# A branch is moved behind the row numbers and the first gather of a routed expert layer, which are then done on a guess

## The chip, the cores and the metric

One Trainium2 chip, one of its cores. The metric is the time of the whole kernel on the device in microseconds (us), the median of several runs.

The core has five engines that work side by side, each in the order of its own instructions: PE (matrix multiplications), DVE (vector operations), ACT (activations and scaled copies), POOL (general vector work, and here the indirect DMAs that gather and scatter rows) and SP (which here issues most of the other DMAs). They wait for one another through semaphores.

## The reference

Attention in blocks, then a layer of eight experts that each take exactly 576 of the 4608 rows.

```python
# q, k, v: 8 x 8 heads x 576 x 64;  block-causal mask of 64
attn = softmax(where(mask, q @ k.T / 8, -1e9)) @ v
x = attn.transpose(0, 2, 1, 3).reshape(4608, 512)

logits = x @ w_gate                     # 4608 x 8
order = argsort(-logits.flatten())      # best pairs of row and expert first
for idx in order:                       # greedy, an expert is full at 576 rows
    tok, e = idx // 8, idx % 8
    if assigned[tok] >= 0 or counts[e] >= 576: continue
    assigned[tok] = e; counts[e] += 1
for e in range(8):
    rows = x[assigned == e]
    out[assigned == e] = relu(rows @ w1[e]) @ w2[e]   # 512 -> 1024 -> 512
```

## The kernel before

The first 330 us or so are attention, which writes x to DRAM as two halves of 16 bits (a high and a low part, 1024 numbers a row). Then come the experts in the order in which they fill up, not in the order of their numbers. For the k-th of them (k from 0 to 7) the class `Moe` does these steps, and those of k+1 lie beside the matrix work of k:

- `route`: a search for the threshold above which exactly 576 pairs lie. A round (`rounds`) counts the pairs above three candidates with DVE and ACT (tiles `jk`, `ja`), sums the counts over the partitions on PE (`tot`) and narrows the interval. For k = 0 it makes 6 rounds, then assumes that the interval is already narrow enough; `bi` says whether that guess is wrong, and a region under `If` does eight more rounds in that case. For k > 0 it makes 14 rounds. `choose` then gives the expert's number (`ei`, as an integer `eidx`) and the mask of its rows (`MM`).
- The end of `route` and `invert`: two scans over the mask, sums on PE, and a row number for every place (`ix`).
- `weights`: SP reads `eidx` into a register and loads this expert's w1 and w2 in eight pieces into six buffers `raw`. ACT makes the high half of each piece, and DVE (k < 2, first four pieces) or POOL (the rest, L991) the low half. A piece may be loaded when the low half of the piece six before it is done.
- `gather`: five indirect DMAs on POOL, m = 0 to 4, fetch 128 rows each (64 for m = 4) into tiles `xg`. `flip` transposes them into X: for k < 2 on PE (`xt`), from k = 2 on by a DMA that SP issues (L1058).
- `ffn`: h = W1 X (L1083), in two halves of the rows, 256 and 320; HH and HL are the high and low half of relu(h); y = HH, HL times W2 (L1109, L1113). POOL scatters the result to its rows (`out_dram`).

A class `Sched` decides the order of the instructions ahead of time. Each step is a generator that yields the engine it needs, an estimated duration in ns, and the events it has to follow; the planner keeps a clock for each engine and takes the step that can start first. It knows only costs and events that are written out; what a tile of a pool waits for is added afterwards as semaphores when a buffer is taken again. `gather` takes `xg` from a pool of five buffers.

The branch for k = 0 is written out by hand: a register load on DVE, PE and ACT, a comparison, and the region (L863, L864). Behind it come the scans (L874), the row numbers, the load of `eidx` on SP (L969) with the first weights, and the first gather. `m_gt` is a small tile that POOL clears behind the first gather (L1032) and DVE writes before its first low half (L979). `m_dg` (L780) is a gather into a tile that nobody reads.

Of the kernel before, what the change touches and what calls it, by code (L numbers as in the profile page):

```python
# [596 lines left out]
class Moe:  # L597
    def __init__(s,tc,nc,ctx,sc,L,xd,w1,w2,out):
        s.tc,s.nc,s.sc,s.L,s.xd,s.w1,s.w2,s.out=tc,nc,sc,L,xd,w1,w2,out
        s.NT=xd.shape[0]; s.D=w1.shape[1]; s.E=w1.shape[0]; s.F=w1.shape[2]; s.CAP=s.NT//s.E; s.C=s.NT//P  # L600
# [4 lines left out]
        s.ab=s.cp.tile([P,1],F32,name="m_ab")
        s.vm=s.cp.tile([P,s.C],F32,name="m_vm"); s.nP=s.cp.tile([P,s.C,s.E],F32,name="m_nP"); s.Lr=s.cp.tile([P,s.C,s.E],F32,name="m_Lr")
        N=s.C*s.E; s.PAD=s.CAP*s.E//P
        s.PB,s.P2=[s.cp.tile([P,N+s.PAD],F32,name=n) for n in ("m_PB","m_P2")]
# [86 lines left out]
    def route(s,k):  # L695
# [10 lines left out]
        SC=rp.tile([P,2,C+1],F16,tag="SC",name=f"SC{k}")  # L706
        eidx=rp.tile([P,1],I32,tag="eidx",name=f"eidx{k}")
        (V if k else nc.gpsimd).memset(SC[:,:,0:1],0.0)
        if last:

# [4 lines left out]
        else:  # L715
# [38 lines left out]
            def rounds(t0,t1):  # L754
                nonlocal lo,nw,PBx,base
                for t in range(t0,t1):
# [91 lines left out]
            else:  # L848

                cg=rp.tile([P,1],F16,name="m_cg",bufs=1); bad=rp.tile([P,2],F32,name="m_bad",bufs=1); bi=rp.tile([P,1],I32,name="m_bi",bufs=1)  # L850
                yield from rounds(0,s.TB)
# [9 lines left out]
                V.scalar_tensor_tensor(bi,tot[:,0:1],float(s.CAP),bad[:,0:1],op0=OP.not_equal,op1=OP.max)  # L861
                ET=mybir.EngineType
                rv=nc.values_load(bi[0:1,0:1],engines=(ET.DVE,ET.PE,ET.Activation),min_val=0,max_val=1)  # L863
                with s.tc.If(rv>0):  # L864
# [6 lines left out]
        nm=1 if last else 2  # L871
        yield D,106*nm
        for i in range(nm):
            V.tensor_tensor_scan(SC[:,i,1:],s.ones[:,:C],MM[:,i],0.0,op0=OP.mult,op1=OP.add)  # L874
        def full():
# [47 lines left out]
    def invert(s,k,L16,h2):  # L923
# [32 lines left out]
        V.tensor_copy(ix,ps[:,:5])  # L956
        sc.set(tk)
        sc.add(s.gather(k,ix),s.PR['gather'],sc.now); sc.set(('ix',k))
        if k==0: sc.add(s.late(),0,sc.now)
        if k==0:  # L960
# [3 lines left out]
            sc.free[T]=max(sc.free[T],sc.now)+213*s.NWU+1500  # L964
        s.ix[k]=ix
    def weights(s,k,eidx):

        nc=s.nc; wp=s.wp; sc=s.sc
        e=nc.sync.value_load(eidx[0:1,0:1],min_val=0,max_val=s.E-1)  # L969
        yield S,1000,('ffn',k-2)  # L970
# [22 lines left out]
        for dst,src,nd,wd in ((W,s.w1,4,1024),(Y,s.w2,8,512)):  # L993
            g=1024//wd
            for d in range(0,nd,g):
# [8 lines left out]
                else: yield S,25,'hw'  # L1004
                if k>1 or n!=4: raw=wp.tile([P,1024],F32,tag="raw",name=f"raw{k}_{wd}_{d}",bufs=6)
                nc.sync.dma_start(out=raw.rearrange("p (g f) -> p g f",g=g),in_=src[bass.ds(e,1),d*P:(d+g)*P,:].rearrange("o (g p) f -> p (o g) f",p=P))  # L1006
                hi=dst[:,0,d:d+g].rearrange("p g f -> p (g f)"); lw=dst[:,1,d:d+g].rearrange("p g f -> p (g f)")
# [12 lines left out]
    def gather(s,k,ix):  # L1020
        nc=s.nc; fp=s.fp; sc=s.sc
        tl=[]
        for m in range(5):
# [4 lines left out]
            nc.gpsimd.indirect_dma_start(out=xg[:n],out_offset=None,in_=s.xd,in_offset=bass.IndirectOffsetOnAxis(ap=ix[:n,m:m+1],axis=0))  # L1028
            sc.soft(728,('xg',k,m))
            sc.nolat()  # L1030
            if k==m==0:
                s.gt=s.rp.tile([P,1],F32,name="m_gt",bufs=1); nc.gpsimd.memset(s.gt,0.0); sc.set(('gt',0))  # L1032
            if m==4: sc.set(('gi',k))
# [144 lines left out]
```

## Time and profile before

| what | value |
|---|---|
| median of 3 runs | 759.99 us (757.54 to 761.68) |
| the profiled execution | 753.41 us, of it 751.6 us the span that the profile shows |
| mean granted clock of PE | 0.982 |
| busy share of the span | PE 94%, DVE 73%, ACT 68%, POOL 51% |

The span is the stretch from the first to the last instruction of the core. The page divides it into 40 slices of 18.8 us; the hand-over from attention to the experts lies in the slices from 325 us on, where PE falls to 6 and 3 tenths. Rows of a timeline give start, duration, engine, line, operation, the tile written and the tiles read, the count of instructions drawn together, and in brackets the idle time of the engine before it and what ended it. SPq, DVEq and so on are the sequencers of the engines. "DMA to landing" is the time from the issue of a transfer until its data have arrived.

### The profile page before, as it was taken

What the parts mean: (1) busy time and instruction counts of PE and PEld (TensorE: products, weight loads), DVE (VectorE), ACT (ScalarE), POOL (GpSimd) and SP (SyncE); (2) the same over time, 40 slices, a digit from 0 to 9 for tenths busy, and PEclk for the clock granted to TensorE, in tenths of its full rate; (3) what the DMA queues carried; (4) which work ended last, traced back from release to release, by engine and by line L of the source; (5) the groups of instructions that cost most, each with busy time, mean ns of one, the idle gap of its engine ahead of it and who ended that gap; (6) DMA issues with size and microseconds to landing.
All of it is one profiled execution on the core that took longest, in us unless ns stands there. A gap on an engine that the chain in (4) does not pass through costs nothing.

```text
span 751.6 us, 18263 instructions
## 1 busy us (share of the span) xinstructions
PE 705.6 (94%) x6314; PEld 455.0 (61%) x6314; DVE 550.6 (73%) x2224; ACT 508.7 (68%) x1378; POOL 380.3 (51%) x455
## 2 busy tenths in 40 slices
PE   5999999999899999637999999999999999999997
PEld 3666776667576766416446647557476475574753
DVE  6999989798887979868989969779587595120210
ACT  5887889888696877427648497694965947474211
POOL 6876564645655562213334276391761834796002
PEclk9999999999999999858999999999999999999999
DMA  9999999999999999745045095673935917993001
GB/s 192 173 200 188 205 214 179 237 179 238 181 238 173 228 202 181 179 141 188 2 169 182 24 305 88 227 167 100 256 80 176 203 38 238 221 260 88 22 15 49
DMA packets 273517, 124.48 MB, mean 166 GB/s; under 512 B 247296, under 2 KB 256512, under 8 KB 273424
## 3 DMA queue, kind: packets, MB, share of 16 engines
q1 hardware_dynamic: 267504, 104.37, 64.9%
q0 software_dynamic: 5920, 18.95, 8.3%
q8 instruction: 49, 0.80, 0.5%
q14 instruction: 44, 0.36, 0.2%
HBM read 71.39 MB, written 18.87 MB: 120 GB/s over the span
## 4 chain that ended last, share of the span: by engine, by line
PE 47%; DMA 3%; issue 3%; ACT 2%; POOL 1%; DVE 1%; SPq 0%; POOLq 0%; ACTq 0%
PE h L1083 24%; PE y L1109 18%; PE y L1113 3%; DMA raw<-in_moe_w_dram 2%; DMA xg<-x,ix 1%; PE pe L944 1%; POOL xg L1028 1%; ACT ja L735 0%; DMA out_dram<-yo,ix 0%; PE xt L1049 0%; PE tot L797 0%; SPq L1006 0%; ACT raw L985 0%; POOL W L991 0%; POOL out_dram L1099 0%
## 5 line engine op out<-in xcount | busy, mean ns | idle before, releaser
L1083 PE MATMUL h<-X,W 128*128 128x320 f16 (+3 forms) x1536 | 194.6, 287 | 0.0
L393 ACT ACTIVATE P<-psb,m 128x576 f32<-128x576 f32 (+8 forms) x288 | 149.5, 546 | 36.9 <-DVE m L389 35.1
L1083 PEld LDWEIGHTS <-W 128*128 128x128 f16 x1536 | 142.6, 98 | 41.9 <-issue 2.6
L991 POOL TENSOR_TENSOR W<-raw,W 128x1024 f16<-128x1024 f32 x56 | 118.4, 2138 | 80.9 <-ACT W L989 61.5
L1109 PE MATMUL y<-W,HH 128*128 128x512 f16 x512 | 152.4, 379 | 0.0
L385 DVE TENSOR_REDUCE m<-psb 128x1 f32<-128x576 f32 (+8 forms) x288 | 124.5, 479 | 10.5 <-PE psb L367 9.8
L437 PE MATMUL psb<-mident,P 128*128 128x128 f32 x800 | 105.5, 279 | 5.3 <-DVE Xf L454 1.9
L437 PEld LDWEIGHTS psb<-mident,P 128*128 128x128 f32 x800 | 85.8, 141 | 24.1 <-ACT P L393 6.8
L1109 PE MATMUL y<-W,HL 128*128 128x512 f16 x256 | 97.0, 379 | 0.0
L1069 ACT ACTIVATE HH<-h 128x320 f16<-128x320 f32 (+3 forms) x128 | 51.7, 411 | 66.9 <-PE h L1083 65.4
L487 PE MATMUL psb<-PT,V 128*64 128x448 f32 (+5 forms) x776 | 96.7, 389 | 0.0
L1099 POOL DMA_INDIRECT out_dram<-yo,ix x40 | 39.1, 978 | 113.3 <-ACT yo L1091 73.9
L367 PE MATMUL psb<-kT,qT 128*64 128x512 f16 (+7 forms) x640 | 85.5, 292 | 3.4 <-DMA qT<-q 1.6
L1071 DVE SCALAR_TENSOR_TENSOR HL<-h,HH 128x320 f16<-128x320 f32 (+3 forms) x128 | 57.2, 453 | 39.1 <-ACT HH L1069 38.6
L418 ACT ACTIVATE PT<-psb 128x512 f32<-128x512 f32 (+1 forms) x157 | 79.4, 580 | 7.3 <-PE psb L437 5.5
L367 PEld LDWEIGHTS <-qT 128*64 128x64 f16 x1280 | 60.8, 110 | 38.5 <-issue 16.6
L1109 PEld LDWEIGHTS <-HH 128*128 128x128 f16 x512 | 46.6, 97 | 52.6 <-issue 1.5
L367 PE MATMUL psb<-kS,qT 128*64 128x512 f16 (+7 forms) x640 | 77.9, 287 | 0.0
L985 ACT ACTIVATE raw<-raw 128x512 f32<-128x512 f32 x112 | 67.8, 627 | 10.6 <-DMA raw<-in_moe_w_dram 10.4
L487 PEld LDWEIGHTS psb<-PT,V 128*64 128x64 f32 x776 | 48.5, 137 | 34.6 <-issue 24.5
L989 ACT ACTIVATE W<-raw 128x512 f16<-128x512 f32 x112 | 68.1, 626 | 0.0
L393 ACT ACTIVATION_READ_ACCUMULATOR P<-psb,m 128x1 f32 x288 | 64.7, 225 | 0.0
(232 smaller groups left out, 1009.7 us busy)
## 6 DMA issues: line engine op xcount, KB each, us to landing
raw<-in_moe_w_dram SPq DMA_DIRECT2D x64, 512.0 KB, 5.0
x<-XR SPq DMA_DIRECT2D x8, 1152.0 KB, 6.7
kn<-in_k_dram SPq DMA_DIRECT2D x15, 576.0 KB, 7.5
qn<-in_q_dram SPq DMA_DIRECT2D x15, 576.0 KB, 7.7
V<-in_v_dram SPq DMA_DIRECT2D x64, 128.0 KB, 2.8
V<-in_v_dram SPq DMA_DIRECT2D x16, 64.0 KB, 2.9
xg<-x,ix POOLq DMA_INDIRECT x40, 4.7
out_dram<-yo,ix POOLq DMA_INDIRECT x40, 3.5
```

Source lines behind the costliest of these rows:

```text
L367: nc.tensor.matmul(ps[64 * h:64 * h + 64, o + a:o + e], lhsT=A[:, h, 64 * i:64 * i + 64], rhs=K[:, h, a:e], start=st, stop=not st)
L385: nc.vector.tensor_reduce(m[:, 0, c:c + 1], ps[:, o:o + 64 * (i + 1)], axis=AX.X, op=OP.max)
L393: nc.scalar.activation(Pt[:, s.OFF[i]:s.OFF[i] + 64 * (i + 1)], ps[:, o:o + 64 * (i + 1)], AF.Exp, bias=m[:, 1, c:c + 1], scale=s.ESC, acc ...
L418: s.nc.scalar.activation(out, in_, AF.Copy)
L437: nc.tensor.transpose(ps[:, a], s.Pb[n % s.NP][:, s.OFF[i] + 128 * j:s.OFF[i] + 128 * j + P], s.ident)
L487: nc.tensor.matmul(ps[64 * h:64 * h + 64, 64 * (i0 - b0):64 * (b1 - b0)], lhsT=vn[:, j, 2 * (n % 2) + h, :], rhs=pt[:, s.PTI[(j, i0)]:s.PT ...
L985: nc.scalar.activation(raw[:,x],raw[:,x],AF.Copy,scale=s.WS)
L989: nc.scalar.activation(hi[:,x],raw[:,x],AF.Copy)
L991: nc.gpsimd.tensor_tensor(lw,raw,hi,op=OP.subtract)
L1071: nc.vector.scalar_tensor_tensor(HL[:,f,ts],ps,0.0,HH[:,f,ts],op0=OP.max,op1=OP.subtract)
L1083: nc.tensor.matmul(ps,lhsT=W[:,a,d,f*P:f*P+P],rhs=X[:,4*(d//2)+d%2+l,ts],start=(d==0 and n==0),stop=(d==3 and n==2))
L1109: if m<4: nc.tensor.matmul(ps,lhsT=Z[:,f,m*P:m*P+P],rhs=Y[:,a,f],start=(f==n==0),stop=(f==7 and n==2))
```

## The change

- For k = 0 the scans, the sums on PE, the row numbers and the first gather no longer stand behind the branch. `eidx` is copied ahead of it, and SP issues the first four weight loads with it.
- The branch (register load and `If`) stands behind `ix`, and now also runs on POOL and SP. POOL's first gather and the clearing of `m_gt` stand ahead of its `If`. The region, for a wrong guess, makes the eight rounds, and then all of this once more: `eidx`, the loads, scans, row numbers and first gather.
- The first gather of k = 0 has a tile of its own (`m_xg0`); the pool `xg` has four buffers in place of five.
- Three small DVE operations (`full`, `used`, `eight`) stand behind the branch; the gather into `m_dg` is gone; the register loads of `eidx` leave out a range check.

```diff
@@ Moe.__init__
+        s.xg0=s.cp.tile([P,1024],F16,name="m_xg0"); s.bi=s.cp.tile([P,1],I32,name="m_bi"); s.e0=s.cp.tile([P,1],I32,name="m_e0")
@@ route, rounds
-                    if k==0 and t==3:
-                        dg=rp.tile([32,1024],F16,name="m_dg",bufs=1)
-                        nc.gpsimd.indirect_dma_start(out=dg,out_offset=None,in_=s.xd,in_offset=bass.IndirectOffsetOnAxis(ap=s.it[:32,P-1:P],axis=0))
@@ route, k == 0
-                yield D,150
+                V.tensor_copy(eidx,ei)
                 V.tensor_tensor(bad[:,0:1],m1[:,6:7],m1[:,1:2],op=OP.not_equal)
+                sc.busy(D,150)
+                yield D,212
+                scans()
+                yield D,100
                 V.scalar_tensor_tensor(bi,tot[:,0:1],float(s.CAP),bad[:,0:1],op0=OP.not_equal,op1=OP.max)
-                ET=mybir.EngineType
-                rv=nc.values_load(bi[0:1,0:1],engines=(ET.DVE,ET.PE,ET.Activation),min_val=0,max_val=1)
-                with s.tc.If(rv>0):
+                yield T,80,'rt'
+                tk=sc.take(); ps=s.ps.tile([P,512],F32,tag="rt",name=f"po{k}")
+                ranks(ps)
+                wg=s.weights(k,eidx)
+                sc.add(wg,s.PR['weights'],sc.now)
+                s.wgo()
+                def redo(e,L16,h2,q):
                     for x in rounds(s.TB,s.NS): pass
                     end()
                     for x in choose(s.NS,0,False): pass
-                for x in (D,T,A): sc.busy(x,1500)
-                yield D,150
-                load()
+                    V.tensor_copy(eidx,ei)
+                    s.fetch(eidx)
+                    scans()
...
@@ invert
+        if k==0:
+            ET=mybir.EngineType
+            rv=nc.values_load(s.bi[0:1,0:1],engines=(ET.DVE,ET.PE,ET.Activation,ET.Pool,ET.SP),min_val=0,max_val=1,skip_runtime_bounds_check_because="a comparison wrote it, so it is 0 or 1")
+            rows=lambda: nc.gpsimd.indirect_dma_start(out=s.xg0,out_offset=None,in_=s.xd,in_offset=bass.IndirectOffsetOnAxis(ap=ix[:,0:1],axis=0))
+            rows()
+            s.gt=s.rp.tile([P,1],F32,name="m_gt",bufs=1); nc.gpsimd.memset(s.gt,0.0)
+            with s.tc.If(rv>0):
+                s.again()
...
+                rows()
+            for x in s.gaps: x()
+            for x in (D,A,G): sc.busy(x,1500)
+            sc.set(('br',0)); sc.set(('gt',0))
         sc.add(s.gather(k,ix),s.PR['gather'],sc.now); sc.set(('ix',k))
@@ weights
-        e=nc.sync.value_load(eidx[0:1,0:1],min_val=0,max_val=s.E-1)
+        if k: e=s.nc.values_load(eidx[0:1,0:1],engines=(mybir.EngineType.SP,),min_val=0,max_val=s.E-1,skip_runtime_bounds_check_because="a one-hot picks it from the numbers 0 to E-1")
+        else:
+            s.raws=[wp.tile([P,1024],F32,tag="raw",name=f"raw0_1024_{d}",bufs=6) for d in range(4)]
+            s.wgo=lambda: s.fetch(eidx)
@@ gather
-            yield G,1038,('ffn',k-2),('xm',k-1,m)
+            if k or m: yield G,1038,('ffn',k-2),('xm',k-1,m)
-            xg=fp.tile([P,1024],F16,tag="xg",name=f"xg{k}_{m}",bufs=5)
-            nc.gpsimd.indirect_dma_start(out=xg[:n],out_offset=None,in_=s.xd,in_offset=bass.IndirectOffsetOnAxis(ap=ix[:n,m:m+1],axis=0))
+            xg=fp.tile([P,1024],F16,tag="xg",name=f"xg{k}_{m}",bufs=4) if k or m else s.xg0
+            if k or m: nc.gpsimd.indirect_dma_start(out=xg[:n],out_offset=None,in_=s.xd,in_offset=bass.IndirectOffsetOnAxis(ap=ix[:n,m:m+1],axis=0))
```

The lists that follow are the order of instructions on an engine in the built program; a name's last number tells tiles of one name apart, and the brackets name the semaphores that an instruction waits for (DMAHW and DMASW are those of transfers).

The branch on SP, at the hand-over. Before, SP reads `eidx` behind the branch of the other engines and then loads the weights:

```order
L512 DMA x<-XR_4825 128x9x512 [waits DMAHW4_49,DMAHW5_49,DMAHW3_49,DMAHW2_49]
L864 UNCONDITIONAL_BRANCH
L969 TENSOR_LOAD eidx_4943 [waits DMAHW2_49,DMAHW3_49,DMAHW1_49,DMAHW4_49,DMAHW0_49,DMAHW5_49,DVE_49,DMAHW6_49,PE_49,DMAHW7_49,Activation_49,Pool_49]
L969 ISA x2
L1006 ISA
L1006 DMA raw_1024_0_5261<-in_moe_w_dram 128x1024 [waits DMAHW6_49,PE_49]
```

Now it reads the guessed number (`m_e`), issues four loads, and only then reads `bi` and branches; the second group of four loads is the region's:

```order
L512 DMA x<-XR_4828 128x9x512 [waits DMAHW4_49,DMAHW5_49,DMAHW3_49,DMAHW2_49]
L1009 TENSOR_LOAD m_e_86 [waits DVE_49]
L1010 ISA
L1010 DMA raw_1024_0_5084<-in_moe_w_dram 128x1024 [waits DMAHW6_49,PE_49]
...
L1010 DMA raw_1024_3_5087<-in_moe_w_dram 128x1024
L977 TENSOR_LOAD m_bi [waits DVE_49]
L981 COMPARE_AND_BRANCH
L1009 TENSOR_LOAD m_e_86 [waits DVE_49]
```

Loads and the number they are addressed by moved ahead of the comparison.

The five gathers of k = 2 on POOL, with the first low half of that expert's weights behind them. Before:

```order
L1028 DMA xg_0_6987<-x,ix_6980 128x1024 [waits DMASW1_49,DVE_49]
L1028 DMA xg_1_7014<-x,ix_6980 128x1024 [waits DMASW2_49,PE_49]
L1028 DMA xg_2_7029<-x,ix_6980 128x1024 [waits DMASW3_49,PE_49]
L1028 DMA xg_3_7047<-x,ix_6980 128x1024 [waits DMASW4_49,PE_49]
L1028 DMA xg_4_7062<-x,ix_6980 64x1024 [waits PE_49]
L991 TENSOR_TENSOR W_2_6846<-raw_1024_0_6865,W_2_6846 128x1024 [waits DMAHW7_49,Activation_49]
```

Now:

```order
L1078 DMA xg_0_7038<-x,ix_7031 128x1024 [waits DMASW1_49,DVE_49]
L1078 DMA xg_1_7065<-x,ix_7031 128x1024 [waits DMASW2_49,PE_49]
L1078 DMA xg_2_7080<-x,ix_7031 128x1024 [waits DMASW3_49,PE_49]
L1078 DMA xg_3_7098<-x,ix_7031 128x1024 [waits DMASW4_49,PE_49]
L1078 DMA xg_4_7113<-x,ix_7031 64x1024 [waits DMAHW5_49,DMASW1_49]
L1039 TENSOR_TENSOR W_2_6897<-raw_1024_0_6916,W_2_6897 128x1024 [waits DMAHW7_49,Activation_49]
```

The rows stand in the same order; the fifth gather now waits for a transfer of SP's, DMAHW5, in place of PE.

The same place on SP, where that transfer and what follows it are issued (now; before, the rows are the same with other line numbers):

```order
L1056 DMA raw_512_2_6958<-in_moe_w_dram 128x2x512 [waits DMAHW6_49,Pool_49]
L1106 DMA_TRANSPOSE X_7037<-xg_0_7038 128x8x128 [waits DMASW1_49,PE_49]
L1056 ISA
L1056 DMA raw_512_4_7173<-in_moe_w_dram 128x2x512 [waits DMAHW7_49,Pool_49]
L1106 DMA_TRANSPOSE X_7037<-xg_1_7065 128x8x128 [waits DMASW2_49]
L1056 ISA
L1056 DMA raw_512_6_7217<-in_moe_w_dram 128x2x512 [waits DMAHW0_49,Pool_49]
```

DMAHW5 is the semaphore of the first transpose, X<-xg_0, and nothing moved in these rows.

More of the change, by code (lines that the diff above doesn't have):

```diff
@@ L706, in route, with scans, ranks @@
         SC=rp.tile([P,2,C+1],F16,tag="SC",name=f"SC{k}")
-        eidx=rp.tile([P,1],I32,tag="eidx",name=f"eidx{k}")
+        eidx=rp.tile([P,1],I32,tag="eidx",name=f"eidx{k}") if k else s.e0
         (V if k else nc.gpsimd).memset(SC[:,:,0:1],0.0)
+        nm=1 if last else 2
+        def scans():
+            for i in range(nm):
+                V.tensor_tensor_scan(SC[:,i,1:],s.ones[:,:C],MM[:,i],0.0,op0=OP.mult,op1=OP.add)
+        def ranks(ps):
+            pos=ps[:,:2*C].rearrange("p (i c) -> p i c",i=2)
+            nc.tensor.matmul(ps[:,:nm*C],lhsT=s.ones,rhs=s.sh[:,:nm*C],start=True,stop=False)
+            nc.tensor.matmul(pos[:,:nm],lhsT=s.tri,rhs=MM[:,:nm],start=False,stop=False)
+            nc.tensor.matmul(pos[:,:nm],lhsT=s.ones,rhs=SC[:,:nm,:C],start=False,stop=last)
+            if not last: nc.tensor.matmul(pos[:,1],lhsT=s.ones,rhs=SC[:,0,C:C+1].to_broadcast([P,C]),start=False,stop=True)
         if last:
@@ L867, in route @@
                     for x in choose(s.NS,0,False): pass
-                for x in (D,T,A): sc.busy(x,1500)
-                yield D,150
-                load()
[L871 to L874, printed above, removed]
+                    V.tensor_copy(eidx,ei)
+                    s.fetch(eidx)
+                    scans()
+                    p2=s.ps.tile([P,512],F32,tag="tot",name="po_")
+                    ranks(p2)
+                    pos=p2[:,:2*C].rearrange("p (i c) -> p i c",i=2); sl=q[:,0]
+                    V.tensor_tensor(q[:,0:2],pos,MM,op=OP.mult)
+                    V.scalar_tensor_tensor(q[:,2],pos[:,1],s.CAP+496.0,MM[:,1],op0=OP.is_lt,op1=OP.mult)
+                    V.tensor_tensor(sl,q[:,0],q[:,1],op=OP.add)
+                    V.tensor_scalar(h2,sl,1.5*2.0**28,1.5*2.0**28,op0=OP.add,op1=OP.subtract)
+                    V.scalar_tensor_tensor(L16,sl,15.5,h2,op0=OP.add,op1=OP.subtract)
+                s.redo=redo
+        if k:
+            yield D,106*nm
+            scans()
         def full():
@@ L880, in route @@
         if not last and k: full()
-        s.hold(k,s.HZ if last else s.HA)
-        yield T,80,'rt',('hold',k)
-        tk=sc.take(); ps=s.ps.tile([P,512],F32,tag="rt",name=f"po{k}")
+        if k:
+            s.hold(k,s.HZ if last else s.HA)
+            yield T,80,'rt',('hold',k)
+            tk=sc.take(); ps=s.ps.tile([P,512],F32,tag="rt",name=f"po{k}")
+            ranks(ps)
         pos=ps[:,:2*C].rearrange("p (i c) -> p i c",i=2)
-        nc.tensor.matmul(ps[:,:nm*C],lhsT=s.ones,rhs=s.sh[:,:nm*C],start=True,stop=False)
-        nc.tensor.matmul(pos[:,:nm],lhsT=s.tri,rhs=MM[:,:nm],start=False,stop=False)
-        nc.tensor.matmul(pos[:,:nm],lhsT=s.ones,rhs=SC[:,:nm,:C],start=False,stop=last)
         q=rp.tile([P,4,C],F32,tag="q",name=f"q{k}")
@@ L910, in route @@
             eight=lambda: V.tensor_scalar(q[:,3],q[:,2],8.0,None,op0=OP.mult)
-            if k==0: s.gaps=[(full,used),(eight,)]
+            if k==0: s.gaps=(full,used,eight); s.again=lambda: s.redo(None,L16,h2,q)
             def out():
@@ L965, in invert, with fetch @@
         s.ix[k]=ix
+    def fetch(s,eidx):
+        e=s.nc.values_load(eidx[0:1,0:1],engines=(mybir.EngineType.SP,),min_val=0,max_val=s.E-1,skip_runtime_bounds_check_because="a one-hot picks it from the numbers 0 to E-1")
+        for d in range(4): s.nc.sync.dma_start(out=s.raws[d],in_=s.w1[bass.ds(e,1),d*P:d*P+P,:].rearrange("o p f -> p (o f)"))
     def weights(s,k,eidx):
         nc=s.nc; wp=s.wp; sc=s.sc
-        e=nc.sync.value_load(eidx[0:1,0:1],min_val=0,max_val=s.E-1)
+        if k: e=s.nc.values_load(eidx[0:1,0:1],engines=(mybir.EngineType.SP,),min_val=0,max_val=s.E-1,skip_runtime_bounds_check_because="a one-hot picks it from the numbers 0 to E-1")
+        else:
+            s.raws=[wp.tile([P,1024],F32,tag="raw",name=f"raw0_1024_{d}",bufs=6) for d in range(4)]
+            s.wgo=lambda: s.fetch(eidx)
         yield S,1000,('ffn',k-2)
@@ L1004, in weights @@
                 else: yield S,25,'hw'
-                if k>1 or n!=4: raw=wp.tile([P,1024],F32,tag="raw",name=f"raw{k}_{wd}_{d}",bufs=6)
-                nc.sync.dma_start(out=raw.rearrange("p (g f) -> p g f",g=g),in_=src[bass.ds(e,1),d*P:(d+g)*P,:].rearrange("o (g p) f -> p (o g) f",p=P))
+                if k>1 or n!=4 and (k or n>3): raw=wp.tile([P,1024],F32,tag="raw",name=f"raw{k}_{wd}_{d}",bufs=6)
+                if k==0 and n<4: raw=s.raws[n]
+                elif k==0 and n==4: e=s.nc.values_load(eidx[0:1,0:1],engines=(mybir.EngineType.SP,),min_val=0,max_val=s.E-1,skip_runtime_bounds_check_because="a one-hot picks it from the numbers 0 to E-1")
+                if k or n>3: nc.sync.dma_start(out=raw.rearrange("p (g f) -> p g f",g=g),in_=src[bass.ds(e,1),d*P:(d+g)*P,:].rearrange("o (g p) f -> p (o g) f",p=P))
                 hi=dst[:,0,d:d+g].rearrange("p g f -> p (g f)"); lw=dst[:,1,d:d+g].rearrange("p g f -> p (g f)")
```

24 lines of the change are left out of this document (15 added, 9 removed).

## The prediction

> **What bounds the kernel now.** I read the page first, then the chain that ended last, then the timelines around the branch, then POOL's and SP's rows expert by expert.
>
> ```profile
> PE 705.6 (94%) x6314; PEld 455.0 (61%) x6314; DVE 550.6 (73%) x2224; ACT 508.7 (68%) x1378; POOL 380.3 (51%) x455
> PE 47%; DMA 3%; issue 3%; ACT 2%; POOL 1%; DVE 1%; SPq 0%; POOLq 0%; ACTq 0%
> ```
>
> PE is busy for 94% of the span, so time is won only where PE idles, and any new PE idle is paid in full. The one long hole of PE lies at the hand-over from attention to the experts, where the branch stands. The timeline of all engines, then POOL, DVE and PE there, in columns of start, duration, engine, line, operation, and idle time before it with what ended it:
>
> ```profile
> 327.98 0.17 DVE L839 TENSOR_TENSOR MM<-ge,MM 128x36 f16<-128x36 f16 x1
> 328.34 0.16 DVE L861 SCALAR_TENSOR_TENSOR m_bi<-m_ct,m_bad 128x1 int32<-128x1 f32 x1
> 330.14 0.15 DVE L752 CAST eidx<-m 128x1 int32<-128x1 f32 x1 [1.63 <-DVEq L864]
> 330.21 0.35 DVE L874 TENSOR_TENSOR_SCAN SC<-m_ones,MM 128x36 f16<-128x36 f16 x2
> 334.95 0.17 DVE L956 CAST ix<-ps 128x5 int32<-128x5 f32 x1 [0.26 <-PE ps L953]
> 335.99 0.98 POOL L1028 DMA_INDIRECT xg<-x,ix  x1 [12.00 <-DMA raw<-in_moe_w_dram]
> 337.27 0.95 POOL L1028 DMA_INDIRECT xg<-x,ix  x1 [0.19 <-issue]
> 337.15 0.06 DVE L979 MEMSET m_gt<- 128x1 f32 x1 [1.68 <-POOL m_gt L1032]
> 341.50 0.62 PE L1049 MATMUL xt<-m_idh,xg 128*128 128x128 f16 x8 [3.08 <-DMA xg<-x,ix]
> ```
>
> The flag is written at 328.34, and DVE stands 1.63 us until its branch falls through; had the region run, many rounds of DVE work would stand there. So the guess holds with these inputs. From the scans to the indices it is 4.7 us (330.21 to 334.95), to the gather 1.0 more, and 5.5 us later PE starts on the gathered rows, the last to arrive.
>
> **The change, part by part. First the branch.** The scans need only MM, which ends at 328.15. With eidx (0.15), the comparison and the flag around them they start at about 328.25 and not 330.21: −2.0 us, and the first weights' addresses come as much earlier. The chain to the first gather is otherwise the same, so that gather goes at about 334.0, PE's first transposes at 339.5. Against it stands the new branch behind ix, now on POOL and SP too:
>
> ```profile
> L863 PEldq TENSOR_LOAD <-m_bi x1: 486/486/486, 328.7 to 328.7; - x1
> L864 PEldq COMPARE_BRANCH  x1: 219/219/219, 329.3 to 329.3; - x1
> L969 SPq FUSED_REGOPS  x8: 152/159/187, 331.0 to 627.6; - x8
> ```
>
> A register load and a branch cost 0.5 + 0.2 us. POOL loads the flag ahead of the first gather, when it has been idle for 12.00 us, so that is hidden; its branch, and the instruction by which it stands in for the region's DMA, come between the first and the second gather. DVE's branch (the 1.63 of before) and the three DVE operations moved behind it (some 1.0 us) lie in DVE's 1.68 us wait at 337.15 and in front of work that waits for data; if that cover is gone, the low halves of the first weights are late by the rest, under 1 us. ACT and SP wait for transfers there. PE must pass the branch before its first transposes, and it has 3.08 us idle. Removing the dummy gather frees POOL inside its 12.00 idle, which gives nothing; should it have warmed something, the first gather would be late by what that was worth, and only its 0.98 against 0.95 of the next hints at it. Front: **−1.7 us**, between −2.4 (with the shorter check as well) and 0 (if POOL's branch costs what DVE's did, later gathers give it all back). The range check that every register load loses is the 0.16 us row, once per expert on SP: −0.2 for those loads that are on the path.
>
> **The tile pool.** In the same diff the gathered rows lose a buffer: the first gather has a tile of its own, and the pool xg goes from five to four. For experts 1 to 7 all five gathers still use the pool. So the fifth, m=4, takes the buffer of the *same* expert's m=0, and must wait until those rows have been transposed; with five it waited for the previous expert's only. For expert 1 PE does this transpose early (nothing). From expert 2 on it is a DMA from SP, and POOL stands in order behind the fifth gather: the low halves of the weights (L991), on which PE waits. The planner's costs don't know it, since the order on POOL stays. What each costs hangs on how long a transpose takes to land. Over all 30, then for experts 2 and 3:
>
> ```profile
> DMA to landing us min/median/max: 2.9/5.4/10.3
> DMA to landing us min/median/max: 4.4/5.1/5.4
> ```
>
> Expert 2, POOL, SP and PE:
>
> ```profile
> 442.07 0.91 POOL L1028 DMA_INDIRECT xg<-x,ix  x1 [0.30 <-issue]
> 443.00 2.14 POOL L991 TENSOR_TENSOR W<-raw,W 128x1024 f16<-128x1024 f32 x1
> 446.35 6.32 POOL L991 TENSOR_TENSOR W<-raw,W 128x1024 f16<-128x1024 f32 x3
> 443.39 1.29 SPq L1058 DMA_TRANSPOSE X<-xg  x1
> 445.17 0.39 SPq L1006 DMA_DIRECT2D raw<-in_moe_w_dram  x1
> 445.61 1.23 SPq L1058 DMA_TRANSPOSE X<-xg  x1
> 452.14 0.83 PE L1083 MATMUL h<-X,W 128*128 128x256 f16 x6
> 452.84 2.78 PE L1083 MATMUL h<-X,W 128*128 128x256 f16 x24
> ```
>
> The first transpose goes out at 443.39, lands 5.1 later, and the gather's 0.30 follows: 448.8 instead of 442.07, +6.7. The four low halves behind it move as one block, since POOL has no gap there: the last ends at 459.4, not 452.67. PE's first group of h (12 matmuls of 0.115) needs it at about 453.4. That is a stall of **6.0 us**; 3.8 if the transpose lands in 2.9, 11.2 if in 10.3. SP is drawn in: its load at 445.17 waits for the low half that ends at 445.14, and the second transpose stands behind that load, so X's second piece lands near 457.4 too. It ends ahead of the low halves and adds nothing.
>
> Experts 3 and 6 have a fifth gather that already waits, or nearly, for that transpose, since other work stands in front: nothing each, at most 2 at expert 6.
>
> ```profile
> 493.49 0.92 POOL L1028 DMA_INDIRECT xg<-x,ix  x1 [0.30 <-DMA X<-xg]
> 640.33 0.91 POOL L1028 DMA_INDIRECT xg<-x,ix  x1 [0.30 <-DMA X<-xg]
> ```
>
> Expert 4, on SP, POOL, ACT and PE:
>
> ```profile
> 535.94 3.45 SPq L1058 DMA_TRANSPOSE X<-xg  x2
> 537.60 0.91 POOL L1028 DMA_INDIRECT xg<-x,ix  x1 [0.30 <-issue]
> 538.53 4.24 POOL L991 TENSOR_TENSOR W<-raw,W 128x1024 f16<-128x1024 f32 x2
> 540.71 0.39 SPq L1006 DMA_DIRECT2D raw<-in_moe_w_dram  x1
> 545.22 0.63 ACT L985 ACTIVATE raw<-raw 128x512 f32<-128x512 f32 x1
> 547.19 0.17 PE L797 MATMUL tot<-cn,m_bo 128*128 128x3 f16 x1
> ```
>
> The gather goes at 535.94 + 5.4 + 0.3 = 541.6, +4.0. The first low half behind it frees the buffer for SP's last load (540.71, just as that half ends), ACT scales that load at 545.22 and does its part of the next expert's count behind it, and PE's sum tot needs that count at 547.19. With about 0.9 slack there, PE stalls **3.1 us** (0.6 for a landing of 2.9).
>
> Expert 5 is the same chain:
>
> ```profile
> 585.97 3.74 SPq L1058 DMA_TRANSPOSE X<-xg  x2
> 587.17 0.92 POOL L1028 DMA_INDIRECT xg<-x,ix  x1 [0.30 <-issue]
> 590.28 0.39 SPq L1006 DMA_DIRECT2D raw<-in_moe_w_dram  x1
> 596.50 0.63 ACT L985 ACTIVATE raw<-raw 128x512 f32<-128x512 f32 x1 [1.82 <-DMA raw<-in_moe_w_dram]
> 597.74 0.17 PE L797 MATMUL tot<-cn,m_bo 128*128 128x3 f16 x1 [0.81 <-ACT ja L735]
> ```
>
> The gather moves by +4.5 (to 585.97 + 5.4 + 0.3), and there is no slack: ACT and PE idle already. But this load took 6.1 us to land, beside the transposes, and a later one may land faster, so I take **3.5** (0.4 to 4.5). Expert 7 has no following expert to count for, and its weights wait long: nothing.
>
> **The clock.** At the hand-over PE was nearly idle, then the granted clock (the column behind POOL) halved. PE's busy time, and that column, in three stretches:
>
> ```profile
> 338.00:341.00 3.00, 0.41 (x1) 0.00 (x0) 3.00 (x4) 1.65 (x3) 2.39 (x3) 0.82 0.88 305
> 344.00:345.00 1.00, 1.00 (x13) 1.00 (x11) 1.00 (x2) 0.00 (x0) 0.00 (x0) 0.50 0.78 201
> 346.00:347.00 1.00, 1.00 (x20) 0.99 (x18) 0.35 (x7) 0.21 (x1) 0.00 (x0) 1.00 0.94 352
> ```
>
> A hole of 3 us here was followed by some 3.4 us at 0.50, worth 1.7 us of work. A hole of 6 us at expert 2 may do that again; the shorter ones may not: **+1.5** in all (0 to 3). The Trainium skill, "TensorE: Matmul & The Clock Gate", Part 1, says the clock halves after an idle window of about 3.4 us that runs freely, and returns after as long a busy one. By that rule a hole of 6 us is sure to hold more than half a window and the two of 3 us are a matter of phase, each worth up to 1.7 us; the rows above agree.
>
> The sum: −1.7 − 0.2 + 6.0 + 3.1 + 3.5 + 1.5 = **+12.2 us**. The profiled execution took 753.41 us (span 751.6, 1.8 around it), 6.6 under the median of 759.99 and below the fastest of its three runs. The sum is a difference, so I add it to the median: 772.2. A change of this kernel that can be told from none is about 0.5%, 3.8 us.
>
> **Rivals.** *Not slower: the transposes are early enough.* The four buffers cost nothing if the fifth gather of expert 2 could go by 442.8, which leaves the last low half in time for 453.4; then only the front's gain remains, 758.1. Against it, the transpose isn't even issued before 443.39, and gathers ahead of it would all have to be faster. For it: the front's shift may alter what meets what on the transfers. Chance 0.09.
>
> *Transposes land fast.* With the trace's least landing, 2.9, the three stalls are 3.8, 0.6 and about 1.5, the clock stays, and with −1.9 the sum is +4.0: 764. For it, the 2.9 occurs; against it, it is the least of 30, and the four to five of experts 2 and 3 lie in 4.4 to 5.4. Chance 0.12. The Trainium skill, "DMA: Bandwidth & Descriptors", gives 2.0 us fixed (Anatomy of one DMA) and 261 GB/s for a transpose (Latency and other measured facts), from which I estimate 3.0 us for the 262 KB of 128 rows; the median of 5.4 disagrees, and by the page's figure this rival would be the forecast.
>
> *The region runs.* A wrong guess would redo at least the chain from flag to gather (328.34 to 335.99, 7.7 us) and eight rounds besides: above 785. The idle of 1.63 speaks against it. Chance 0.02.
>
> *POOL's stand-in instruction is slow.* It would hold gathers two to five by some 2 us, and turns −1.7 into 0: inside the range.
>
> **How the numbers follow.** The forecast has 0.77, with 764 to 780 of its own: low, 3.8 + 0.6 + 0.4 less 2.6 gives +2.2, which the fast rival shares; high, all landings at 7, the clock's 3 and no front gain give +20. The 80% range is 760 to 780: below it lies the first rival and little else. Faster by over 0.5% (under 756.2) needs the first rival with a large front gain: 0.04. Within 0.5% (to 763.8): the rest of that rival and almost half of the fast one: 0.12. Slower: 0.84.
>
> **What would show it.** In the profile after: the first gather near 334.0 and the first transposes on PE near 339.5 (front right); on POOL at expert 2 a fifth gather with 4 to 7 us idle, ended by the transpose X<-xg, and PE idle 4 to 6 us at the first h of that expert; PE idle about 3 us before a tot at experts 4 and 5, released by ACT, with the transposes behind the gather's wait there too; a granted clock of 0.5 behind the first of these holes. Wrong would be: fifth gathers without idle, or with idle that PE doesn't show because the low halves have slack I didn't see; or a first gather no earlier than 335.9.

## The result, and the profile after

| | median | runs | range |
|---|---|---|---|
| before | 758.76 us | 4 | 757.28 to 761.68 |
| changed | 768.22 us | 4 | 764.21 to 770.00 |

Slower: ratio 1.0103, 95% interval 1.0074 to 1.0133, that is +9.5 us on the medians, where +12.2 was forecast. In the experiments below, in another set of runs, the changed kernel had 770.5 and the kernel before 753.6, ratio 1.023 (1.020 to 1.026), +16.9. The changed kernel repeats within 2.3 us, the kernel before doesn't (758.8 here, 753.3 to 754.6 in four later sets); why is open. The two profiled executions (753.41 and 770.00) differ by 16.6, so what the traces show is to be held against the larger figure.

The page after, its engines and the first line of the chain that ended last:

```profile
PE 710.9 (93%) x6314; PEld 456.7 (59%) x6314; DVE 549.8 (72%) x2224; ACT 509.9 (66%) x1378; POOL 380.8 (50%) x454
PE 42%; DMA 6%; issue 3%; POOL 2%; DVE 2%; ACT 1%; SPq 0%; POOLq 0%; ACTq 0%; DVEq 0%
```

Transfers have twice their share of the chain, and POOL twice its own: something waits for a DMA through POOL. The view of the tile xg on SP names it; it counts who waited for the transposes (us, times). Before, POOL waited 0.6 us in two places:

```profile
  POOL xg L1078: 16.9, 4
```

The front in the changed kernel's timeline (L713 are the scans, L973 the indices, L978 the first gather, L1078 the others, L1097 PE's transposes):

```profile
327.49 0.35 DVE L713 TENSOR_TENSOR_SCAN SC<-m_ones,MM 128x36 f16<-128x36 f16 x2
332.26 0.17 DVE L973 CAST ix<-ps 128x5 int32<-128x5 f32 x1 [0.35 <-PE ps L970]
332.72 1.18 POOL L978 DMA_INDIRECT m_xg<-x,ix  x1 [14.28 <-DVE ix L973]
333.59 0.16 DVE L900 TENSOR_TENSOR m_es<-m_es,m 128x1 f32<-128x1 f32 x1 [1.16 <-DVEq L981]
334.36 0.96 POOL L1078 DMA_INDIRECT xg<-x,ix  x1 [0.33 <-POOL m_gt L980]
337.85 0.62 PE L1097 MATMUL xt<-m_idh,m_xg 128*128 128x128 f16 x8 [0.73 <-DMA m_xg<-x,ix]
```

It is 3.3 us earlier at the gather and 3.65 at PE; 0.7 of that is attention, which ended earlier in this execution (MM at 327.28, not 327.98). The branch on POOL shows as 0.33 us ahead of the second gather, 0.14 more than before.

Expert 2, on POOL, SP and PE (L1039 is the low half, L1106 the transpose, L1131 is h):

```profile
448.04 0.90 POOL L1078 DMA_INDIRECT xg<-x,ix  x1 [4.83 <-DMA X<-xg]
448.95 2.15 POOL L1039 TENSOR_TENSOR W<-raw,W 128x1024 f16<-128x1024 f32 x1
452.32 6.29 POOL L1039 TENSOR_TENSOR W<-raw,W 128x1024 f16<-128x1024 f32 x3
443.40 1.30 SPq L1106 DMA_TRANSPOSE X<-xg  x1
451.58 1.23 SPq L1106 DMA_TRANSPOSE X<-xg  x1
457.13 1.46 PE L1131 MATMUL h<-X,W 128*128 128x256 f16 x6 [3.49 <-DMA X<-xg]
```

POOL stands 4.83 us at the fifth gather. PE's hole ends with the *second* transpose, which SP could only issue at 451.58 since the load ahead of it waited for the late low half.

Experts 3, 4 and 5: the fifth gather on POOL, and for 4 and 5 the sum tot on PE, in a short and a long hole (for 5 with SP's late load and ACT's scaling of it, L1033, ahead of the long one):

```profile
501.77 0.91 POOL L1078 DMA_INDIRECT xg<-x,ix  x1 [1.82 <-DMA X<-xg]
549.41 0.90 POOL L1078 DMA_INDIRECT xg<-x,ix  x1 [5.11 <-DMA X<-xg]
547.10 0.18 PE L805 MATMUL tot<-cn,m_bo 128*128 128x3 f16 x1 [0.60 <-ACT yo L1139]
557.81 0.16 PE L805 MATMUL tot<-cn,m_bo 128*128 128x3 f16 x1 [2.69 <-ACT ja L746]
602.57 0.91 POOL L1078 DMA_INDIRECT xg<-x,ix  x1 [5.09 <-DMA X<-xg]
600.32 0.18 PE L805 MATMUL tot<-cn,m_bo 128*128 128x3 f16 x1 [0.63 <-ACT yo L1139]
605.67 0.39 SPq L1056 DMA_DIRECT2D raw<-in_moe_w_dram  x1
610.47 0.63 ACT L1033 ACTIVATE raw<-raw 128x512 f32<-128x512 f32 x1 [3.92 <-DMA raw<-in_moe_w_dram]
611.71 0.16 PE L805 MATMUL tot<-cn,m_bo 128*128 128x3 f16 x1 [3.36 <-ACT ja L746]
```

The clock, by stretches, behind the holes of experts 2 and 5. A row has the stretch, its length, the busy time of PE, PEld (PE's weight loads), DVE, ACT and POOL, and then the granted clock, the busy share of the DMA engines and their GB/s:

```profile
454.00:457.00 3.00, 0.00 (x0) 0.00 (x0) 0.15 (x1) 1.51 (x4) 3.00 (x3) 0.98 1.14 346
457.00:460.00 3.00, 2.87 (x15) 2.06 (x16) 1.98 (x9) 1.28 (x4) 2.62 (x2) 0.50 1.14 286
610.00:612.00 2.00, 0.29 (x2) 0.13 (x2) 0.09 (x2) 1.53 (x4) 2.00 (x2) 0.62 1.12 219
612.00:614.00 2.00, 2.00 (x6) 0.60 (x4) 1.69 (x11) 1.24 (x4) 2.00 (x2) 0.50 0.99 181
614.00:616.00 2.00, 2.00 (x11) 0.55 (x11) 0.00 (x0) 1.51 (x3) 1.83 (x2) 0.50 0.00 0
616.00:618.00 2.00, 2.00 (x14) 0.94 (x16) 1.71 (x10) 0.69 (x3) 0.41 (x1) 0.68 0.32 131
```

Behind expert 4's hole it stayed at 1.00. In the traces of this case the time between two changes of the granted clock is always a multiple of 3.41 us; behind the holes here it stays halved for one or two such steps. Cut along these steps, expert 4's hole of 2.69 us falls into two of them (the first two rows), expert 5's mostly into one:

```profile
552.44:555.86 3.42, 2.68 (x14) 1.10 (x13) 1.62 (x10) 0.89 (x2) 3.22 (x4) 1.00 0.64 161
555.86:559.27 3.41, 1.46 (x9) 0.56 (x10) 1.15 (x8) 2.69 (x7) 3.41 (x2) 1.00 1.17 231
607.06:610.47 3.41, 1.28 (x6) 0.49 (x5) 0.81 (x5) 0.00 (x0) 3.21 (x3) 1.00 0.96 202
610.47:613.88 3.41, 2.17 (x7) 0.73 (x6) 1.78 (x11) 2.77 (x7) 3.41 (x3) 0.50 1.14 214
613.88:617.29 3.41, 3.41 (x17) 1.09 (x17) 1.15 (x8) 2.20 (x5) 2.36 (x2) 0.50 0.11 43
```

A step with 1.46 us of PE's work left the clock full, and behind one with 1.28 us it was halved. It stayed so behind a step with 2.17 us of work and came back after a full one.

Laid side by side by the start of each expert's first gather, the time goes as follows (us between the first gathers of successive experts, from POOL's rows in the trace of each run; "0" is from MM to the first gather, the last column from expert 7's first gather to the end):

| kernel | 0 | 0→1 | 1→2 | 2→3 | 3→4 | 4→5 | 5→6 | 6→7 | 7→end |
|---|---|---|---|---|---|---|---|---|---|
| before | 8.0 | 53.4 | 47.6 | 48.1 | 46.1 | 49.6 | 50.6 | 28.3 | 91.9 |
| changed | 5.4 | 58.3 | 47.5 | 53.4 | 46.4 | 53.2 | 56.6 | 28.7 | 91.5 |
| changed, again (experiment 4) | 5.4 | 54.8 | 48.9 | 53.6 | 46.1 | 54.0 | 54.5 | 28.0 | 92.2 |
| before, four buffers | 8.0 | 53.4 | 47.1 | 53.4 | 46.1 | 56.2 | 56.0 | 34.2 | 88.9 |
| changed, shared tile | 5.4 | 58.0 | 48.1 | 49.1 | 46.1 | 49.7 | 49.7 | 31.4 | 89.1 |
| the same, weights planned later | 5.4 | 54.1 | 46.7 | 49.3 | 45.5 | 50.8 | 49.7 | 30.8 | 89.5 |

The changed kernel gains 2.6 us to the first gather, loses 4.9 behind it, and then 5.3, 3.6 and 6.0 at experts 2, 4 and 5. What 6→7 loses comes back behind 7, wholly or in part, in several kernels and not by the edit. The loss of 4.9 right behind the front was not forecast. ACT before (L730 copies m_PB, L985 scales the load of w2):

```profile
347.29 0.38 ACT L730 ACTIVATE m_PB<-rt 128x256 f32<-128x256 f32 x1
347.55 0.63 ACT L985 ACTIVATE raw<-raw 128x512 f32<-128x512 f32 x1
```

Now:

```profile
346.61 0.63 ACT L1033 ACTIVATE raw<-raw 128x512 f32<-128x512 f32 x1 [3.50 <-DMA raw<-in_moe_w_dram]
347.14 0.37 ACT L741 ACTIVATE m_PB<-rt 128x256 f32<-128x256 f32 x1
347.54 0.51 DVE L787 TENSOR_SCALAR_CACHE_REDUCE jk<-m_PB,bs 128x288 f16<-128x288 f32 x1 [4.21 <-ACT m_PB L741]
348.56 0.19 PE L805 MATMUL tot<-cn,m_bo 128*128 128x3 f16 x1 [2.54 <-DVE jk L787]
350.69 0.48 PE L1131 MATMUL h<-X,W 128*128 128x128 f16 x3 [1.60 <-DVE HL L1119]
```

ACT's order differs there. Before, it copied m_PB (needed by the next expert's count) and then scaled the first piece of w2; now the scaling stands first and waits 3.50 us for its load, m_PB behind it, DVE's count behind that, and PE behind the count.

### The profile page after: what moved, and what is told of

Same layout as the page of the kernel before. It is cut to its first block, busy times and chain, and to the rows that moved or that the text cites. A ratio compares the mean times of both kernels' runs of the same rounds, so it can differ in the third digit from the quotient of the medians.

```text
span 768.2 us, 18256 instructions
## 1 busy us (share of the span) xinstructions
PE 710.9 (93%) x6314; PEld 456.7 (59%) x6314; DVE 549.8 (72%) x2224; ACT 509.9 (66%) x1378; POOL 380.8 (50%) x454
## 4 chain that ended last, share of the span: by engine, by line
PE 42%; DMA 6%; issue 3%; POOL 2%; DVE 2%; ACT 1%; SPq 0%; POOLq 0%; ACTq 0%; DVEq 0%
PE h L1131 25%; PE y L1157 13%; DMA X<-xg 3%; PE y L1161 3%; DMA raw<-in_moe_w_dram 2%; DMA xg<-x,ix 1%; POOL xg L1078 1%; POOL W L1039 1%; PE pe L963 1%; PE tot L805 0%; DVE jk L787 0%; SPq L1056 0%; DMA out_dram<-yo,ix 0%; ACT ja L746 0%; ACT W L1025 0%
## 5 line engine op out<-in xcount | busy, mean ns | idle before, releaser
L1131 PE MATMUL h<-X,W 128*128 128x320 f16 (+3 forms) x1536 | 197.2, 289 | 5.1 <-DMA X<-xg 3.5
L1131 PEld LDWEIGHTS <-W 128*128 128x128 f16 x1536 | 144.4, 99 | 46.7 <-DMA X<-xg 4.0
L1039 POOL TENSOR_TENSOR W<-raw,W 128x1024 f16<-128x1024 f32 x56 | 118.4, 2138 | 87.0 <-ACT W L1037 72.1
L1157 PEld LDWEIGHTS <-HH 128*128 128x128 f16 x512 | 46.7, 98 | 57.9 <-issue 7.6
L1033 ACT ACTIVATE raw<-raw 128x512 f32<-128x512 f32 x112 | 67.2, 622 | 18.3 <-DMA raw<-in_moe_w_dram 18.1
```

The costliest lines, as they stand in the source:

```text
L1033: nc.scalar.activation(raw[:,x],raw[:,x],AF.Copy,scale=s.WS)
L1039: nc.gpsimd.tensor_tensor(lw,raw,hi,op=OP.subtract)
L1131: nc.tensor.matmul(ps,lhsT=W[:,a,d,f*P:f*P+P],rhs=X[:,4*(d//2)+d%2+l,ts],start=(d==0 and n==0),stop=(d==3 and n==2))
L1157: if m<4: nc.tensor.matmul(ps,lhsT=Z[:,f,m*P:m*P+P],rhs=Y[:,a,f],start=(f==n==0),stop=(f==7 and n==2))
```

## The experiments

Each kernel was timed in five rounds beside the kernel before (three rounds for the two with a forced flag); the ratio is to that.

**1. Four buffers alone.**

```diff
 # kernel before
-            xg=fp.tile([P,1024],F16,tag="xg",name=f"xg{k}_{m}",bufs=5)
+            xg=fp.tile([P,1024],F16,tag="xg",name=f"xg{k}_{m}",bufs=4)
```

> The kernel before with one edit: the pool xg has four buffers, the branch stays where it was. Theory A (the four buffers carry the change's cost): slower than before by 8 to 14 us; on POOL the fifth gathers of experts 2, 4 and 5 wait 4 to 5 us for the transpose, PE has a hole of about 3.5 us at the first h of expert 2 and of about 3 us at a tot of experts 4 and 5, as the changed kernel has. Theory B (the moved branch and what it rearranges carry it): within 3 us of before, and the waits on POOL don't reach PE.

770.22 against 753.63 us, ratio 1.0217 (1.0188 to 1.0247), +16.6. All of the loss comes from this one number; the order of instructions is the same on every engine, only waits differ. Its views of the tile on SP (who waited for the transposes) and of PE's waits (us, times, longest):

```profile
  POOL xg L1028: 21.3, 5
...
PE tot L797 <- ACT ja L735: 10.5, 3, 4.9
PE h L1083 <- DMA X<-xg: 3.9, 1, 3.9
```

Theory A holds; it ends a little above the range's upper end.

**2. The changed kernel with the fifth gather in the first gather's tile.**

```diff
 # changed kernel
-            xg=fp.tile([P,1024],F16,tag="xg",name=f"xg{k}_{m}",bufs=4) if k or m else s.xg0
+            xg=fp.tile([P,1024],F16,tag="xg",name=f"xg{k}_{m}",bufs=4) if (m<4 if k else m) else s.xg0
```

> The changed kernel with one edit: for experts 1 to 7 the fifth gather uses the first gather's own tile, so that no expert waits for its own first transpose; no tile more than in the changed kernel. Theory A: the holes at experts 2, 4 and 5 go, 8 to 12 us less than the changed kernel, and what is left is the front, where the first transposes come 3 us earlier and ACT's wait for a weight load gives that back: between -2 and +2 us of before. Theory B: it stays 6 us or more above before.

753.79 against 753.63, ratio 1.0003 (0.9987 to 1.0018): 16.7 us under the changed kernel, with no tile more. No gather waits for a transpose any more. At expert 2 PE still waits 1.20 us for the second transpose, which took 7.8 us from its issue. The profiled execution took 757.87, 4.1 above the median, so its row in the table is not a typical one. In it the front's gain is still missing; ACT's wait and the clock behind it:

```profile
348.41 0.63 ACT L1033 ACTIVATE raw<-raw 128x512 f32<-128x512 f32 x1 [3.06 <-DMA raw<-in_moe_w_dram]
...
350.00:353.00 3.00, 1.03 (x10) 0.88 (x11) 2.88 (x17) 3.00 (x12) 0.00 (x0) 0.50 0.24 94
```

**3. The same, with the first expert's w2 planned to arrive 4 us later.**

```diff
 # on top of 2
                 if k==1 and n>3: sc.ev['wl',k,n]+=s.WL
+                if k==0 and n>3: sc.ev['wl',k,n]+=4000
```

> As the run with the shared tile, and the planner is told that the second-layer weights of the first expert arrive 4 us later, which puts ACT's copy m_PB and the first count ahead of the scaling of that load. Theory A (ACT, standing in front of that load, eats the front's gain): PE's holes of 2.5 and 1.6 us behind the first transposes shrink by at least 2 us together, and the kernel is 2 to 5 us under before. Rival (the front is limited by the second-layer weights or by DVE anyway): within 1.5 us of the shared-tile run.

751.29 against 753.63, ratio 0.9972 (0.9954 to 0.9990), −2.3: faster than both kernels. The edit only changes the planner's estimate; ACT now copies m_PB as soon as it is there:

```profile
343.64 0.38 ACT L741 ACTIVATE m_PB<-rt 128x256 f32<-128x256 f32 x1
```

From MM to expert 1's first gather it takes 59.6 us, before 61.4, changed kernel 63.7 in one execution and 60.2 in the other (experiment 4). But with this estimate ACT and DVE have another order than in experiment 2 at some fifty places each, as late as expert 4 (555 us), so the gain can't be put down to m_PB alone. With 2.5 us in place of 4 the order differs in the first expert's stage only (348 to 378 us):

> The shared-tile kernel with the second-layer weights of the first expert planned 2.5 us later in place of 4: ACT's copy m_PB still stands ahead of the scaling of the load, but the scaling stands ahead of three of the first four HH. If only the place of m_PB matters, it is as the run with 4 us, -1 to -3.5 us of before; if the place of HH matters as well (PE waits for HL to free its results' banks), it lies between that and the shared-tile run, 0 to -1.5.

752.48 against 753.33, ratio 0.9983 (0.9967 to 1.0000), −0.9. In its trace m_PB comes early as well, and MM to gather takes 59.3 us, as short. This is the narrower test of the order at the front: by the ratios some 1.5 us less than experiment 2, with intervals that overlap. The medians lean to the second reading, the trace to the first; the place of HH is undecided.

**4. The changed kernel again, beside these.**

> The changed kernel as it is, for a comparison on the same chip as the three others: both theories expect 6 to 12 us over before, with the three holes and a halved clock behind some of them.

770.5 against 753.63, ratio 1.0230 (1.0200 to 1.0260), above the range given. Its ACT waited only 0.53 us for the load of w2, so 0→1 took 54.8 us, not 58.3: the front's loss varies from one execution to the next. The three holes of PE are there again, 3.70, 2.77 and 3.17 us long; in the first execution they were 3.49, 2.69 and 3.36.

**5. One expert's hole at a time.** The fifth gather gets a tile of its own in the kernel before, except at the experts named; there it takes the buffer of the first.

```diff
 # kernel before; (4,5) in the second one
+        s.xg4=s.cp.tile([P,1024],F16,name="m_xg4")
-            xg=fp.tile([P,1024],F16,tag="xg",name=f"xg{k}_{m}",bufs=5)
+            xg=s.xg4 if m==4 and k not in (2,) else fp.tile([P,1024],F16,tag="xg",name=f"xg{k}_{m}",bufs=4)
```

> The kernel before, with a tile of its own for every fifth gather except expert 2's, which takes the buffer of expert 2's first. The price of expert 2 alone. By the prediction's terms +6.0 for the hole and +1.5 for the clock; by the profile of the changed kernel a hole of 3.5 plus 1.5 of halved clock, +5. If the three holes only cost together (through what each does to the next), +0 to 2.

> The same, but the recycled buffer at experts 4 and 5 only. By the prediction's terms +6.6 without the clock; by the profile of the four-buffer kernel two holes of 3 to 5 us at tot and a halved clock behind at least one of them, +9 to 11. This and the run for expert 2 should add up to the four-buffer kernel's +16.6; less than 13 in sum would mean that something else in the four buffers costs.

759.26 against 754.63, ratio 1.0053 (1.0029 to 1.0078), about +4.0 by the ratio; and 763.93, ratio 1.0127 (1.0091 to 1.0163), +9.6. The sum is 13.6, with some 4 us of uncertainty, against 16.6; the four-buffer kernel also waits at experts 3 and 6 (1.3 and 1.9 us on POOL). Expert 2's hole costs by itself, and so do those of 4 and 5; expert 2's is nearer to the +5 of the profile than to the prediction's +7.5.

**6. A wrong guess.** The flag compares the count with 577, so that the region always runs.

```diff
-...(bi,tot[:,0:1],float(s.CAP),bad[:,0:1],...)
+...(bi,tot[:,0:1],float(s.CAP+1),bad[:,0:1],...)
```

> The kernel before, with the flag forced (it compares the count with 577), so that the region runs; the result is the same. Price of a wrong guess there: eight rounds of some 1.6 us and a choice of 3.5, +13 to 20.

> The shared-tile kernel with the late weights, with the flag forced in the same way, so that rounds, loads, scans, row numbers and the first gather are done twice. Theory (the region lies on the path, the guess's work is thrown away): the rounds as before plus the chain from flag to gather a second time, +22 to 32 over before. Rival (the loads of the guess already warm or block nothing, the redone loads are hidden): no more than the kernel before with the forced flag, +13 to 20.

771.20 and 770.75 against 754.63, +16.6 and +16.1 (ratios 1.0237 and 1.0204, intervals overlap). The first real gather, in the kernel before with the forced flag and in the shared-tile kernel with it:

```profile
351.39 0.98 POOL L1028 DMA_INDIRECT xg<-x,ix  x1 [28.10 <-DMA raw<-in_moe_w_dram]
...
355.04 0.96 POOL L978 DMA_INDIRECT m_xg<-x,ix  x1 [20.44 <-DVE ix L995]
```

My theory was wrong. The real gather comes 3.7 us later in the second (2.9 from the flag, which stood at 327.59 and 328.35), and not by the 7.7 of a whole chain: the flag's branch only waits out the guessed chain, and the chain behind the region is there in both kernels. In the total nothing of it is seen.

**7. The small removals.** The dummy gather and the range checks, taken out of the kernel before; then the checks alone; then both put back into kernel 3.

```diff
-                    if k==0 and t==3:
-                        dg=rp.tile([32,1024],F16,name="m_dg",bufs=1)
-                        nc.gpsimd.indirect_dma_start(out=dg,...)
...
-        e=nc.sync.value_load(eidx[0:1,0:1],min_val=0,max_val=s.E-1)
+        e=s.nc.values_load(eidx[0:1,0:1],engines=(mybir.EngineType.SP,),...,skip_runtime_bounds_check_because="...")
```

> The kernel before with only the small removals of the change: no gather into m_dg, no range check on the loads of the expert's number. The prediction priced them at 0 and -0.2; if the dummy gather warms something for the first real one, the first gather would last longer than 0.98 us (the changed kernel's took 1.18) and the kernel would be up to 0.5 us slower. Within 1 us of before in both cases.

> The kernel before with the range checks of the expert's number removed and the dummy gather kept. The run with both removed was 2.3 us slower. If the checks' removal did it (loads reach their queue some 0.2 us sooner and meet other transfers), this one is +1 to +3.5 too; if the dummy gather did it, this one is within 1 us of before.

> The shared-tile kernel with the late weights, with the dummy gather and the range checks put back: the moved branch alone. If those two removals cost 2.3 us here as they did in the kernel before, 3 to 6 us under before (the run without them was 2.3 under); if what they cost hangs on how the transfers of the kernel before happen to meet, the same 1 to 3.5 us under as without them.

755.19 against 753.33, ratio 1.0031 (1.0015 to 1.0046), +2.3 by the ratio and more than the 1 us expected; checks alone 754.05 against 753.75, 1.0016 (0.9998 to 1.0034); kernel 3 with both back 752.20, 0.9976 (0.9961 to 0.9992), as without them. The first gather without a dummy ahead of it takes 1.18 us instead of 0.98, in every kernel of this study without it:

```profile
335.62 1.18 POOL L1025 DMA_INDIRECT xg<-x,ix  x1 [16.94 <-DMA raw<-in_moe_w_dram]
```

That is 0.2 us, and the rest of the 2.3 is not in that trace, whose span (750.7) is even shorter than before's. Since putting both back gained nothing in kernel 3, it isn't a price of the operations that carries over; where it comes from stays open.

## Why the prediction was right, point by point

- **The tile pool, +12.6 forecast without the clock.** The mechanism was right: experiment 1 has the whole loss with nothing else changed, experiment 2 takes it away.
- **Expert 2, +6.0.** The stage takes 5.3 us longer with its clock loss in it (5.3 as well in experiment 5), so the term was too large; the hole is 3.5. The step that failed is the gather's delay, +6.7: it was +4.5 (4.83 us idle in place of 0.30). The gathers stood 1.4 us later here (the fourth at 442.25, before at 440.82), but the first transpose went out as early as before (443.40 and 443.39); and from its issue to the gather it took 4.6, not 5.4. Less the slack of 0.7 that the prediction had, that leaves 3.8. I also let the last low half end the wait, with the second transpose 2 us ahead of it. It was the second transpose that ended it, and behind it the halved clock slowed PE's first products (1.46 us for six, not 0.83), so that the low halves were in time. That made little of the size: in the execution of experiment 4 the clock was still full there, and PE waited another 0.18 us for a low half.
- **Experts 4 and 5, +3.1 and +3.5.** The stages take 3.6 and 6.0 longer in the changed kernel, but these two terms, which are without the clock, were about right. From the first transpose's issue to the fifth gather it took 6.7 us (542.75 to 549.41) and 7.3 (595.26 to 602.57), where I had 5.7, and the gather came 4.8 later at both (I had 4.0 and 4.5). PE's holes are 2.69 and 0.60 at expert 4, where there was none before, and 3.36 and 0.63 at expert 5, where there was one of 0.81: +3.3 and +3.2. The short ones are missing in the execution of experiment 4, and their cause is open. "A later one may land faster" held at expert 5: from the load's issue to ACT it took 4.8 us, before 6.2. The rest of the 6.0 is the clock.
- **The clock, +1.5 in all.** Too small. At expert 2 it is about 1.6 by itself (one step of 3.4 us at 0.50); at expert 5 the four stretches from 610 to 618 lack 0.38, 0.50, 0.50 and 0.32 of their 2 us, 3.4 in all, some 0.6 of it while PE was idle anyway. Behind expert 4 it didn't fall, but in the second execution of the changed kernel (experiment 4) a hole as long, 2.77 us, lay in one step (PE busy for 0.85 us of it) and was followed by stretches of 3 us at 0.85 and 0.59. So the clock's answer hangs on where a hole of this length falls, not on its length alone. Hole and clock together give the stage: at expert 5 the second execution has a hole 2.4 us longer than before and one step at half rate, 1.7, and the stage takes 3.9 longer (54.5 against 50.6). The rule that the prediction took from the Trainium skill ("TensorE: Matmul & The Clock Gate", Part 1), a free-running window of about 3.4 us, agrees with the steps of 3.41 us. That a whole window must be idle, as the Trainium skill has it there, doesn't agree: a step with 1.28 us of work in it halved the clock. Its return after one busy window fits expert 2 and expert 5, where the first step at half rate held only 2.17 us of work and the second was full.
- **Experts 3 and 6, nothing.** Right: +0.2 and +0.4.
- **The front, −1.7.** To the first gather it was −2.6, more than forecast, because the gather also followed ix 0.6 us sooner than before. But at expert 1 it had turned into +2.3 (63.7 against 61.4 from MM) in the profiled execution; in that of experiment 4 it was −1.2, near the forecast. The step that failed is "ACT and SP wait for transfers there": I priced the branch on ACT and didn't see that behind it the planner had put the scaling of a load ahead of m_PB. The trace shows the wait. That the order costs the kernel time is borne out by experiment 3, but not proved: with m_PB early the front is −1.9 and −2.1 from MM to expert 1, and −2.3 and −0.9 in the whole, the first with other changes of order, the second with an interval that reaches 1.
- **The dummy gather, 0 and the checks, −0.2.** The first gather's 0.2 us, which I only hinted at, is real. No gain of the checks was seen.
- **The rivals.** *Not slower*: the transpose was issued at 443.40 and the gather behind it went at 448.04, far from in time. *Fast landing*: 4.6 to 7.3 us from issue to the gather, no 2.9; my estimate of 3.0 us from the Trainium skill ("DMA: Bandwidth & Descriptors") doesn't fit these three places. The 2.0 us of fixed cost that the Trainium skill gives there ("Anatomy of one DMA") are measured on DMAs that GpSimd (POOL) issues; the transposes come from SP. *The region runs*: it did not; its price, put at "above 785", is +16.6 in the kernel before and some 19 in kernel 3 (751.3 and 770.75, from two sets), so below that. *POOL's stand-in*: 0.14 us, not 2.
- **The size as a whole.** +12.2 lies between +9.5 and +16.9, and which of the two holds is open. Against the profiled execution the clock was 2.9 too small and the front, with its 0.2 for the checks, 4.2, while expert 2's hole was some 2.4 too large. That these cancel in part is luck; the places and the waits were not.

## What to carry to other kernels

A buffer taken from a pool isn't priced by its bytes: count, for each tile that will reuse a buffer, who frees it and what stands behind the waiting instruction on its engine. Here the fifth of five gathers waited for its own expert's first transpose, and the weight conversions behind it, which have nothing to do with the gather, carried that to TensorE; a tile that was free from then on took the holes of experts 4 and 5 away and most of expert 2's. When a step comes earlier, look again at the order behind it on the engines that were not meant to be touched: a planner that believes that a load is there sooner will put its user in front of work that could have run.

## What the runs showed of the hardware that was not expected

- The first indirect DMA of a kernel took longer on POOL: 1.18 us where the first real gather was the first, in seven traces, and 0.98 or 0.99 where the dummy had gone ahead, in seven others, even 29 us ahead (experiment 6).
- The clock's answer to a hole of PE varies. Two executions of the changed kernel had holes of 2.7 and 2.8 us at expert 4, one with no fall of the granted clock and one with some 3 us at half rate; at expert 5 holes of 3.4 and 3.2 us were followed by almost 7 us at half rate in one and by 3 in the other. In these traces it is decided in steps of 3.41 us, and a step need not be idle throughout: 1.46 us of PE's work kept the clock full at expert 4, with 1.28 us it was halved at expert 5. There is no sharp limit by PE's busy time: at the front, steps with 1.8 us of work went both ways (337.40 to 340.82 and 344.23 to 347.64). A hole of 3 us so costs 3 to 6 us.
